# Choosing the rows of expert tiles with SyncE's registers instead of VectorE's tables, and new durations for the planner of the instruction order

## The chip, the cores and the metric

The kernel runs on one core of a Trainium2 chip. The metric is the device time of one execution in microseconds. A core has five engines with an instruction queue each: TensorE (PE; its weight loads are listed as PEld), VectorE (DVE), ScalarE (ACT), GpSimd (POOL) and SyncE (SP). Each works through its own queue in order, and they meet through semaphores. SyncE computes nothing on tensors: here it starts nearly all DMAs and has registers, on which its queue does whole-number arithmetic. GpSimd starts the indirect DMAs (scatters).

## The reference

A dynamic convolution is followed by a top-1 mixture of experts. The input x is (8, 3584, 192), in 8 heads of 24 columns; there are 8 experts with 1024 hidden columns.

```python
w = softmax(weight_gen)                         # (8, 3584, 8 heads, 7 taps)
attn[b, s, h, :] = sum_k w[b, s, h, k] * x_padded[b, s + k, h, :]
x = attn.reshape(28672, 192)
logits = x @ w_gate                             # 8 experts
e_idx = argmax(logits, axis=1)
gate_w = softmax(logits)[e_idx]
eom = 1 / (1 + exp(-(x @ w_output_gate)))
for e in range(8):
    mask = e_idx == e
    out[mask] = gate_w * eom[mask, e] * (relu(x[mask] @ w1[e]) @ w2[e])
```

Each row goes to one expert, so the rows of an expert have to be brought together before its matrix products, and how many there are is known only while the kernel runs.

## The kernel before

**The front.** The 28,672 rows are cut into 32 units of 896 rows (128 partitions of 7 rows, line 232 to 234). For a unit, softmax_steps (line 544) makes the seven weights of a row and head on VectorE and ScalarE. Seven products x times weight follow (product, line 532): five on GpSimd (tile gap) and two on VectorE for most units. From unit 7 on VectorE adds them up in PSUM (acc_steps, line 612: the add ps<-ps,gap for a product of GpSimd, ps<-ps,vt for one of its own); for the first seven units TensorE does it with an identity matrix. sum_steps (line 680) splits the sum into two float16 halves (tile rt), turns it with seven DMA transposes (tile gt, from unit 6 on), and TensorE makes the logits; lz is VectorE's read of them. Then VectorE finds the expert and TensorE the rank of each row among the rows of its expert (tile rk: columns 0 to 7 the rows ahead in the unit, columns 8 to 15 the unit's count for each expert). place_steps (line 835) adds the running total of each expert (tile base), and GpSimd scatters the 896 rows in seven indirect DMAs to a buffer in DRAM (srtd), in which each expert has 32,768 rows of its own.

**The tiles.** tile_steps (line 982) and tile_load (line 1003) load tiles of 512, 384, 256 or 128 rows of one expert: meta (row numbers and scales), xT (the rows, transposed by the DMA), and the expert's weights in float16 halves (wa or late, and wb). TensorE multiplies by w1 (gemm1_unit, line 1018); ScalarE takes relu into hh and VectorE the rest into hl (evac_steps, line 1031), which frees the PSUM bank; TensorE multiplies by w2 (gemm2_group, line 1040), ScalarE scales into ys, and GpSimd scatters to the output.

**Which tile comes next.** How many tiles of which size are taken after which unit is fixed when the kernel is written (plan_rounds, line 27): 76 tiles with 29,312 rows. Which expert a tile is of depends on the data. round_table (line 878) works that out on VectorE, on one partition: for R tiles of T rows it makes the 8 x R table of "expert e has T rows more" (gg), a running sum of it limited to R (cs), which of the R tiles is which expert's (ge), the first row of each (ti, row 1) and the expert's number by a shift of the row (ti, row 0, line 925). tile_load reads both numbers from SBUF into SyncE's registers with value_load (lines 1005 and 1006). After the last unit, VectorE also counts the 128-row tiles that are still left for a loop behind the planned ones (line 947).

**The waits.** A tile load must come after the scatters that write its rows. In before it waits for all scatters that stand ahead of it in the order (list(state["writers"]), line 997).

**The order.** Each engine's queue is written out by hand by a small planner. Every step of the work is a generator, a Chain with a rank and a time; Order.step (line 88) goes on with the chain that can start first, by rank among equals. Paced (line 138) and Queue (line 107) wrap the engines: each call adds the instruction and advances the engine's planned time by a duration from vector_cost, scalar_cost, gpsimd_cost, tensor_cost and sync_cost (lines 178 to 213), n being the elements of a partition. So these numbers are nothing that the chip sees, but they set in what order the instructions stand in each queue. Two tiles at a time are loaded ahead while the front runs (AHEAD, line 1260), four afterwards.

**The end.** When all 32 units are through, tile pools are exchanged, more PSUM banks are given to the products, and the tiles that are left run by themselves. Eight DMAs write a block of empty rows behind each expert's rows (pad, line 994).

Of the kernel before, what the change touches and what calls it, by code (L numbers as in the profile page):

```python
# [11 lines left out]
F32 = mybir.dt.float32  # L12
I32 = mybir.dt.int32
AF = mybir.ActivationFunctionType
ALU = mybir.AluOpType
# [5 lines left out]
RMAX = 24  # L21
SHIFT = 15
NE = 8
# [32 lines left out]
def constants():  # L56

    ident = np.eye(P, dtype=np.float32)
    upper = np.triu(np.ones((P, P), np.float32), 1)
    r = np.arange(RMAX, dtype=np.float32)  # L60
    rr = np.tile(r[:, None], (1, 9))
    need = [T * r for T in (128, 256, 384, 512)]
    e8 = np.arange(8, dtype=np.float32) - 8.0
    flat = np.concatenate([rr.ravel(), *need, e8]).astype(np.float32)
    return np.concatenate([ident, upper, np.tile(flat[None], (P, 1))], axis=1)
# [41 lines left out]
class Queue:  # L107
# [6 lines left out]
    @property  # L114
    def t(self):
        if self.host is not None:
            return self.host.t
        return max(self.moved, self.issued + self.lead)

# [86 lines left out]
def sync_cost(name, args, kwargs):  # L206
# [6 lines left out]
    return n / 360e3 * (1.25 if name == "dma_start_transpose" else 1.0)  # L213
# [4 lines left out]
def kernel(ctx: ExitStack, tc: tile.TileContext, x, wg, wgate, wogate, w1, w2, cst, out):  # L218
# [69 lines left out]
    f_mx = few[:, 80:136]  # L288
    f_lim = few[0:1, 189:190]

    f_next = few[0:1, 136:152].rearrange("p (e r) -> p e r", r=2)
    f_z = few[0:1, 152:170].rearrange("p (e r) -> p e r", r=2)
    f_done = f_next[:, :, 0]
    f_ex = ps[:, 2536:2538].bitcast(I32)
    f_rr = ps[0:1, 2512 : 2512 + RMAX]

    rest_free = [(0.0, 3904), (0.0, 1344)]
    mx_free, few_free, sq_free = [0.0], [0.0], [0.0]
# [44 lines left out]
    cf = cp.tile([P, cst.shape[1]], F32, name="cf")  # L343
    nc.scalar.dma_start(out=cf, in_=cst)
# [14 lines left out]
    o = 256  # L359
    rr = cf[0:1, o : o + RMAX * 9].rearrange("p (a b) -> p a b", b=9)  # L360
    o += RMAX * 9
    need = {}
    for k in (128, 256, 384, 512):
        need[k] = cf[0:1, o : o + RMAX]
        o += RMAX
    nc.vector.tensor_copy(f_e8, cf[:, o : o + 8])
# [3 lines left out]
    for e in range(NE):  # L370
        nc.vector.memset(base[:, e : e + 1], float(e * CAP - 1))
        nc.vector.memset(f_done[:, e : e + 1], float(e * CAP))


    cs = cp.tile([1, 1 + 8 * RMAX], F32, name="cs")
    nc.vector.memset(cs[:, 0:1], 0.0)
    nc.vector.memset(f_z[:, 8, :], float(DUMMY))
    nc.vector.tensor_copy(f_rr, rr[:, :, 0])
# [9 lines left out]
    state = {"base": base, "writers": [], "t": 0, "weights": 0, "rounds": 0}  # L388

# [154 lines left out]
    def softmax_steps(u):  # L544

        w4 = wloads[u]
        mxb = f_mx.unsqueeze(2).broadcast_to([P, NV, K])
        yield from take(mx_free, V)
# [21 lines left out]
        mx_free.append(od.cur.t)  # L570
# [109 lines left out]
    def sum_steps(u):  # L680
# [84 lines left out]
        od.add(place_steps(u), (RANK_C, u, 0), V)  # L765

# [67 lines left out]

    def place_steps(u):
# [11 lines left out]
        d["rk_home"].append((od.cur.t, d["rk_at"]))  # L847
        d["ranked"] = True
        if u in plan:
            od.add(round_steps(u), (RANK_R, u), V)  # L850
        else:
            state["rounds"] += 1
# [20 lines left out]
        d["sent"] = True  # L873
        d["sent_t"] = od.cur.t + 2.5
        rt_free.append((d["sent_t"], d["ri"]))


    def round_table(r, T, R, tail, bs):

        nm = f"{r}"  # L880
        rT = need[T][:, 0:R].unsqueeze(1).broadcast_to([1, 8, R])
        if R > 2:
            n = R
            nx = sp.tile([1, 8, RMAX], F32, tag="nx", bufs=1, name=f"nx{nm}")[:, :, 0:R]
            z = sp.tile([1, 9, RMAX], F32, tag="z", bufs=1, name=f"z{nm}")[:, :, 0:R]
            V.memset(z[:, 8, :], float(DUMMY))
            V.tensor_tensor(out=nx, in0=f_done.unsqueeze(2).broadcast_to([1, 8, R]), in1=rT, op=ALU.add)
            state["step"] = None
            yield V
        else:  # L890
            if state.get("step") != T:
                state["step"] = T if R == 2 else None
                if R == 2:
                    V.tensor_scalar(f_next[:, :, 1], f_done, float(T), None, op0=ALU.add)
                    yield V
            n = 2 if state["step"] == T else 1
            nx, z = f_next[:, :, 0:n], f_z[:, :, 0:n]

        gg = sp.tile([1, 8 * RMAX], F32, tag="gg", bufs=1, name=f"gg{nm}")[:, 0 : 8 * R]
        V.scalar_tensor_tensor(out=gg.rearrange("p (e r) -> p e r", r=R), in0=bs[0:1, :].unsqueeze(2).broadcast_to([1, 8, R]), scalar=0.0 if tail else 1.0 - T, in1=nx[:, :, 0:R], op0=ALU.add, op1=ALU.is_ge)  # L900
        yield V

        if state.get("limit") != R:
            V.memset(f_lim, float(R))
            state["limit"] = R
        V.tensor_tensor_scan(out=cs[:, 1 : 1 + 8 * R], data0=gg, data1=f_lim.broadcast_to([1, 8 * R]), initial=0.0, op0=ALU.add, op1=ALU.min)
        yield V
        cx = cs[:, 0 : 1 + 8 * R : R]

        V.scalar_tensor_tensor(out=z[:, 0:8, :], in0=cx[:, 0:8].unsqueeze(2).broadcast_to([1, 8, n]), scalar=-float(T), in1=nx, op0=ALU.mult, op1=ALU.add)  # L910
        ge = sp.tile([1, RMAX, 9], F32, tag="ge", bufs=1, name=f"ge{nm}")[:, 0:R, :]
        V.tensor_tensor(out=ge, in0=cx.unsqueeze(1).broadcast_to([1, R, 9]), in1=f_rr[:, 0:R].unsqueeze(2).broadcast_to([1, R, 9]), op=ALU.is_le)
        yield V
        n = 1 if R > 2 else n
        V.scalar_tensor_tensor(out=f_next[:, :, 0:n], in0=cx[:, 1:9].unsqueeze(2).broadcast_to([1, 8, n]), scalar=float(T), in1=z[:, 0:8, 0:n], op0=ALU.mult, op1=ALU.add)
        V.tensor_tensor(out=ge, in0=ge, in1=z[:, :, 0:R].rearrange("p e r -> p r e"), op=ALU.mult)
        yield V
        if R > 8:
            ti = sp.tile([1, 2, RMAX], I32, tag="til", bufs=1, name=f"ti{nm}")
        else:  # L920
            ti = sp.tile([1, 2, 8], I32, tag="ti", bufs=NU // 2 + 6, name=f"ti{nm}")
        with nc.allow_low_precision(reason="whole numbers"):
            V.tensor_reduce(out=ti[:, 1, 0:R], in_=ge, axis=AX, op=ALU.max)
        yield V
        V.tensor_scalar(ti[:, 0, 0:R], ti[:, 1, 0:R], SHIFT, None, op0=ALU.arith_shift_right)
        yield V
        return ti
# [3 lines left out]
    def round_steps(u):  # L931

        found, bs = [], U[u]["base"]
        yield V, lambda: state["rounds"] == u
        for k, (T, R) in enumerate(plan[u]):
            tail = u == NU - 1 and k == len(plan[u]) - 1
            pads = None
            if tail:
                pads = sp.tile([1, NE], I32, tag="bi", name="bi")
                bf = sp.tile([1, NE], F32, tag="bf", name="bf")  # L940
                V.tensor_scalar(bf, bs[0:1, :], 1.0, None, op0=ALU.add)
                yield V
                V.tensor_copy(pads, bf)
            ti = yield from round_table(f"{u}_{k}", T, R, tail, bs)
            for i in range(R):
                found.append((T, ti, i, pads if i == 0 else None))
        if u == NU - 1:

            more = sp.tile([1, NE], F32, tag="more", bufs=1, name="more")
            state["done"] = cp.tile([1, NE], F32, name="done")  # L950
            V.tensor_copy(state["done"], f_done)
            V.tensor_tensor(out=more, in0=bs[0:1, :], in1=f_done, op=ALU.subtract)
            yield V
            V.tensor_scalar(more, more, 128.0, None, op0=ALU.add)
            yield V
            morei = sp.tile([1, NE], I32, tag="morei", bufs=1, name="morei")
            V.tensor_copy(morei, more)
            yield V
            V.tensor_scalar(morei, morei, 7, None, op0=ALU.arith_shift_right)
            yield V  # L960
            V.tensor_copy(more, morei)
            yield V
            left = sp.tile([1, 1], F32, tag="left", bufs=1, name="left")
            V.tensor_reduce(out=left, in_=more, axis=AX, op=ALU.add)
# [338 lines left out]
```

## Time and profile before

| what | value |
|---|---|
| times of three runs | 1226.5, 1228.21, 1228.29 us; median 1228.21 |
| profiled execution: time, span | 1230.08 us, 1228.0 us |
| mean granted TensorE clock | 0.974 |
| VectorE shift ti<-ti: shortest, median, longest | 129, 170, 3364 ns |
| DMA issues on SyncE: transposes gt, tiles xT | 182, 76 |
| HBM over the span | 194 GB/s |

How to read it: the span runs from the first to the last instruction of the profiled execution. "Busy" is the time in which an engine had an instruction running; a busy TensorE need not be at its full rate, for which the granted clock stands. A row such as `PE ps <- DVE hl: 34.4, 38, 2.6` says that TensorE stood idle ahead of instructions on the tile ps until an instruction of VectorE on hl ended: us in total, times, longest. In the timeline, the number in brackets is the idle time ahead of an instruction and what ended it; neighbouring instructions of one kind are merged (x5). Nearly all instructions have the line of a helper (L151, L125), so the tiles' names tell them apart: out<-in. SPq is SyncE's queue.

### The profile page before, as it was taken

How to read it: one execution, taken by the hardware profiler on the slowest of the kernel's cores; microseconds unless marked ns; L12 is line 12 of the kernel's file. 1: busy time of each engine (PE TensorE's matmuls, PEld its weight loads, DVE VectorE, ACT ScalarE, POOL GpSimd, SP SyncE). 2: the span in 40 equal slices, each digit the busy share in tenths (PEclk: the TensorE clock that was granted, in tenths of full speed). 3: DMA queues.
4: the chain of work that ended last, by engine and by line, in shares of the span. 5: the costliest groups of instructions: out<-in, count | busy, mean ns of one | idle time of the engine just before them, and what ended most of it. 6: DMA issues, size and time to landing. Idle time of an engine off the chain costs nothing.

```text
span 1228.0 us, 27900 instructions
## 1 busy us (share of the span) xinstructions
PE 1132.9 (92%) x9710; PEld 821.3 (67%) x9710; DVE 956.4 (78%) x2027; ACT 594.5 (48%) x1263; POOL 879.8 (72%) x778
## 2 busy tenths in 40 slices
PE   5988779899999999899999999899998999999997
PEld 2444448677666666676766666676666777988987
DVE  6898759899999898998998999899998663333331
ACT  3875345455555445454544454445544544344342
POOL 5668786668888788888888988888887663322222
PEclk9998989899999999999999999999999999999999
DMA  9998378999989869698769759997777679889992
GB/s 281 284 283 288 131 237 196 262 277 250 247 232 240 206 182 248 150 262 211 213 191 229 208 154 244 231 234 188 207 203 185 178 219 278 235 255 330 272 310 80
DMA packets 278047, 279.73 MB, mean 228 GB/s; under 512 B 211479, under 2 KB 236808, under 8 KB 277905
## 3 DMA queue, kind: packets, MB, share of 16 engines
q1 hardware_dynamic: 256016, 233.35, 69.1%
q0 software_dynamic: 21744, 44.30, 13.3%
q8 instruction: 76, 1.25, 0.4%
q14 instruction: 67, 0.54, 0.1%
q10 hardware_dynamic: 144, 0.29, 0.1%
HBM read 177.07 MB, written 60.87 MB: 194 GB/s over the span
## 4 chain that ended last, share of the span: by engine, by line
PE 40%; DVE 26%; POOL 12%; issue 8%; DMA 7%; SPq 3%; ACT 3%; POOLq 0%; DVEq 0%; ACTq 0%
PE ps L151 40%; DVE ps L151 11%; POOL gap L151 6%; DVE hl L151 5%; POOL srtd L151 3%; SPq L125 3%; DMA srtd<-rt,posi 2%; POOL out_dram L151 2%; DMA wa<-wd 2%; DVE rt L151 2%; DMA gt<-rt 1%; DVE vap L151 1%; ACT rt L151 1%; DVE ti L151 1%; DVE vt L151 1%
## 5 line engine op out<-in xcount | busy, mean ns | idle before, releaser
L151 PE MATMUL ps<-xT,wa 128*128 128x512 f16 (+3 forms) x2440 | 493.0, 350 | 42.7 <-DVE hl L151 33.3
L151 PE MATMUL ps<-wb,hh 128*128 128x192 f16 x3664 | 478.9, 248 | 4.8 <-DVE hl L151 4.8
L151 PE MATMUL ps<-wb,hl 128*128 128x192 f16 x1832 | 454.1, 248 | 0.1
L151 DVE SCALAR_TENSOR_TENSOR hl<-ps,hh 128x512 f16<-128x512 f32 (+1 forms) x472 | 307.5, 665 | 156.3 <-ACT hh L151 155.9
L151 POOL TENSOR_TENSOR gap<-x,w 128x960 f32<-128x960 f32 (+5 forms) x268 | 360.0, 1368 | 37.1 <-DVE lz L151 9.2
L151 ACT ACTIVATE hh<-ps 128x512 f16<-128x512 f32 (+1 forms) x472 | 272.1, 582 | 226.1 <-PE ps L151 223.5
L151 PEld LDWEIGHTS <-wa 128*128 128x128 f16 x2440 | 226.5, 99 | 226.7 <-issue 48.8
L151 PEld LDWEIGHTS <-hh 128*128 128x128 f16 x3664 | 337.0, 99 | 50.5 <-issue 9.4
L151 POOL DMA_INDIRECT out_dram<-ys,meta x216 | 214.5, 993 | 193.6 <-ACT ys L151 146.3
L151 POOL DMA_INDIRECT srtd<-rt,posi x224 | 229.0, 1022 | 87.0 <-issue 56.4
L151 DVE TENSOR_TENSOR ps<-ps,gap 128x1344 f32<-128x1344 f32 x125 | 194.2, 1554 | 21.8 <-POOL gap L151 21.8
L151 ACT ACTIVATE ys<-ps,sc 128x192 f32<-128x192 f32 x229 | 96.3, 421 | 221.0 <-PE ps L151 160.5
L151 PEld LDWEIGHTS <-hl 128*128 128x128 f16 x1832 | 180.9, 99 | 0.6 <-DVE hl L151 0.3
L151 PE MATMUL ps<-gap,cf 128*128 128x512 f32 x168 | 72.9, 569 | 3.2 <-DVE vap L151 3.2
L151 PE MATMUL ps<-vap,cf 128*128 128x512 f32 (+1 forms) x126 | 58.2, 603 | 13.5 <-DVE vap L151 12.9
L151 POOL TENSOR_TENSOR gap<-halo,w 128x1152 f32<-128x1152 f32 (+4 forms) x38 | 60.4, 1589 | 13.2 <-issue 5.7
L151 DVE SCALAR_TENSOR_TENSOR rt<-ps,sx,rt 128x448 f16<-128x448 f32 x64 | 57.9, 908 | 10.4 <-ACT rt L151 5.8
L151 PE MATMUL ps<-xT,late 128*128 128x128 f16 (+2 forms) x600 | 56.6, 251 | 0.0
L151 ACT ACTIVATE rt<-ps 128x1344 bf16<-128x1344 f32 x32 | 41.3, 1291 | 28.2 <-issue 18.3
L151 PEld LDWEIGHTS ps<-gap,cf 128*128 128x128 f32 x168 | 31.4, 199 | 34.8 <-issue 25.6
L151 PEld LDWEIGHTS ps<-vap,cf 128*128 128x128 f32 x126 | 24.9, 208 | 38.7 <-issue 22.9
L151 ACT ACTIVATE rt<-ps,sx 128x1344 f16<-128x1344 f32 x32 | 44.2, 1380 | 9.6 <-DVE isx L151 7.6
(123 smaller groups left out, 841.8 us busy)
## 6 DMA issues: line engine op xcount, KB each, us to landing
wb<-wd SPq DMA_DIRECT2D x76, 768.5 KB
wa<-wd SPq DMA_DIRECT2D x61, 768.0 KB
x<-in_x_dram SPq DMA_DIRECT2D x32, 672.0 KB
late<-wd SPq DMA_DIRECT2D x15, 768.0 KB
wa<-wd SPq DMA_DIRECT2D x61, 128.0 KB
w<-in_wg_dram SPq DMA_DIRECT2D x32, 196.0 KB
wd<-wpb SPq DMA_DIRECT2D x8, 768.5 KB
st<-in_w_dram SPq DMA_DIRECT2D x8, 768.0 KB
```

Of the source, the lines that this page charges most:

```text
L125: r = f(*args, **kwargs)
L151: r = f(*args, **kwargs)
```

## The change

Five things change.

1. SyncE keeps one register for each expert: key[e] = (rows waiting << 11) + (first row / 128). After each unit, ScalarE writes the unit's eight counts, times 2048, as whole numbers to SBUF (count_steps); SyncE loads them and adds them to the keys (counted).
2. pick(T) takes the largest of the eight keys, so the expert with most rows waiting, or an empty tile if no expert has T rows, moves that expert's key on by T rows, and leaves the first row in a register for tile_load. round_table and VectorE's closing count are gone; end_of writes the blocks of empty rows, and turns_left counts the tiles left, which come back through one DMA from a table of numbers.
3. A tile load waits for the scatters up to the unit for which it was picked (U[u]["writers"]), not for all that stand ahead of it.
4. The planner's durations for VectorE, ScalarE, GpSimd and the DMAs are new, and it counts SyncE's register work (spend).
5. softmax_steps has two places for f_mx in PSUM instead of one, and the table of constants is 264 columns wide when loaded.

The plan of sizes, the ranks and the other constants stay. The diff, cut to its core:

```diff
 def vector_cost(name, args, kwargs):
     n = largest(args, kwargs)
-    return 0.06 + n / 156.0 if name == "reciprocal" else 0.07 + n / 960.0
+    return 0.15 + n / 156.0 if name == "reciprocal" else 0.15 + n / 960.0
...
 def scalar_cost(name, args, kwargs):
-    return (0.19 if "accum_out" in kwargs else 0.1) + largest(args, kwargs) / 1200.0
+    own = max(0.2, 0.12 + largest(args, kwargs) / 1050.0)
+    return own + (0.2 if "accum_out" in kwargs else 0.0) + (0.0 if isinstance(kwargs.get("scale", 1.0), float) else 0.1)
...
 def gpsimd_cost(name, args, kwargs):
     if name == "indirect_dma_start":
-        return 1.2 if LOCK else 1.04
+        return 1.28
...
-    return (0.14 if LOCK else 0.06) + largest(args, kwargs) * (0.0022 if kwargs.get("op") == ALU.add else 0.00174)
+    return 0.19 + largest(args, kwargs) * (0.0022 if kwargs.get("op") == ALU.add else 0.00178)
...
-    return n / 360e3 * (1.25 if name == "dma_start_transpose" else 1.0)
+    return n / 310e3 * (1.5 if name == "dma_start_transpose" else 1.0)
...
+    def counted(cnt):
+        R.reg_load(came, cnt[0:1, 0:NE])
+        for e in range(NE):
+            R.reg_alu(key[e], key[e], came[e], ALU.add)
+        SP.spend(0.6)
+
+    def pick(T):
+        R.reg_mov(best, (T - 1 << HAVE) + (DUMMY >> ROW))
+        for e in range(NE):
+            R.reg_alu(best, best, key[e], ALU.max)
+        for e in range(NE):
+            R.reg_alu(came[e], key[e], best, ALU.is_ge)
+            R.reg_alu(came[e], came[e], (T >> ROW) - (T << HAVE), ALU.mult)
+            R.reg_alu(key[e], key[e], came[e], ALU.add)
+        R.reg_alu(best, best, low, ALU.bitwise_and)
+        SP.spend(1.1)
+        return R.snap(best, min_val=0, max_val=DUMMY >> ROW)
...
+    def count_steps(u):
+        cnt = U[u]["cnt"] = sp.tile([1, NE], I32, tag="cnt", bufs=CNT, name=f"cnt{u}")
+        S.activation(cnt, U[u]["rk"][0:1, 8:16], AF.Copy, scale=float(1 << HAVE))
+        rank_read(u)
...
-    def round_table(r, T, R, tail, bs):
...
     def round_steps(u):
-        found, bs = [], U[u]["base"]
-        yield V, lambda: state["rounds"] == u
...
-            ti = yield from round_table(f"{u}_{k}", T, R, tail, bs)
+        yield SP, lambda: state["rounds"] == u and "counted" in U[u]
+        od.cur.t = max(od.cur.t, U[u]["counted"])
+        yield SP
+        counted(U[u]["cnt"])
+        found, subs = [], [(T, k) for k, (T, n) in enumerate(plan.get(u, ())) for _ in range(n)]
+        for T, k in subs:
...
+            yield SP
+            found.append((T, pick(T), u))
...
-            d = tile_load(state["t"], T, ti, i, list(state["writers"]), ka, kb)
+            d = tile_load(state["t"], T, at, U[u]["writers"], ka, kb)
...
-        e = SP.value_load(ti[0:1, 0, i : i + 1], min_val=0, max_val=NE - 1)
-        row = SP.value_load(ti[0:1, 1, i : i + 1], min_val=0, max_val=DUMMY + 4 * P - T)
+        R.reg_alu(hit, at, SHIFT - ROW, ALU.logical_shift_right)
+        e = R.snap(hit, min_val=0, max_val=NE - 1)
+        row = at * (1 << ROW)
```

More of the change, by code (lines that the diff above doesn't have):

```diff
@@ L59, in constants @@
     upper = np.triu(np.ones((P, P), np.float32), 1)
[L60 to L62 removed]
     e8 = np.arange(8, dtype=np.float32) - 8.0
[L64 removed]
+    turns = np.arange(TURNS, dtype=np.int32).view(np.float32)
+    flat = np.concatenate([e8, turns])
     return np.concatenate([ident, upper, np.tile(flat[None], (P, 1))], axis=1)
@@ L873, in place_steps @@
         d["sent"] = True
+        d["writers"] = list(state["writers"])
         d["sent_t"] = od.cur.t + 2.5
         rt_free.append((d["sent_t"], d["ri"]))
-    def round_table(r, T, R, tail, bs):
[L880 to L927, printed above, removed]
@@ L947, in round_steps @@
-        if u == NU - 1:
[L949 to L964, printed above, removed]
-            yield V
-            lefti = state["left"] = sp.tile([1, 1], I32, tag="lefti", bufs=1, name="lefti")
-            V.tensor_copy(lefti, left)
@@ L968, in round_steps @@
-        state["rounds"] += 1
+        yield SP, lambda: state["rounds"] == u and "counted" in U[u]
[4 more added lines that the diff above has]
+        for T, k in subs:
+            if u == NU - 1 and k == len(plan[u]) - 1 and "ended" not in state:
+                state["ended"] = True
+                for e in range(NE):
+                    yield SP
+                    end_of(e)
+                    od.cur.t = od.now
+            yield SP
+            found.append((T, pick(T), u))
@@ L1280 @@
 GT = 1
+CNT = 4
 TR_U = 6
```

108 lines of the change are left out of this document (53 added, 55 removed).

## The prediction

> **What bounds the kernel now.** I read the page first, then the busy times by stage, the chain, the waits of each engine in the middle stage, and at last the timeline around single stalls.
>
> ```profile
> span 1228.0 us, 27900 instructions
> PE 1132.9 (92%) x9710; PEld 821.3 (67%) x9710; DVE 956.4 (78%) x2027; ACT 594.5 (48%) x1263; POOL 879.8 (72%) x778
> ```
>
> Busy times by stage (us, then busy us and instructions of PE, PEld, DVE, ACT, POOL; granted clock; DMA):
>
> ```profile
> 260.00:960.00 700.00, 660.01 (x5704) 471.56 (x5702) 652.56 (x1361) 345.36 (x773) 602.83 (x529) 0.98 0.82 214
> 0.00:260.00 260.00, 212.78 (x1251) 132.44 (x1252) 205.36 (x472) 139.84 (x264) 183.25 (x153) 0.93 0.85 249
> ```
>
> The last long piece of the chain:
>
> ```profile
> 963.13 254.02 PE ps L151 x2694
> ```
>
> The kernel ends in 254.02 us of TensorE without a break, so a backlog of tiles is there when the front (attention, routing) stops. The time is therefore TensorE's work plus TensorE's idle time plus what the slow clock costs. A front that merely runs faster gains nothing; only removed gaps on TensorE do. They lie ahead of 963 us: 260 - 212.78 = 47 us idle in the first stage, 700 - 660.01 = 40 us in the middle one, and a granted clock of 0.93 and 0.98, worth up to 0.07 x 260 = 18 and 0.02 x 700 = 14 us.
>
> What TensorE waits for in the middle stage (us, times, longest):
>
> ```profile
> PE ps L151 <- DVE hl L151: 34.4, 38, 2.6
> ```
>
> So 34.4 of the 40 us are VectorE's second half of an evacuation (hl, line 1034) coming late. VectorE is busy 652.56 of 700 us and runs in order: what stands ahead of an hl delays TensorE. Two things do. The first is the last operation of a routing table (line 925):
>
> ```profile
> 500.86 3.36 DVE L151 TENSOR_SCALAR ti<-ti 1x2 int32<-1x2 int32 x1
> 501.49 2.70 POOL L151 TENSOR_TENSOR gap<-x,w 128x576 f32<-128x576 f32 x2
> 504.14 1.55 DVE L151 TENSOR_TENSOR ps<-ps,gap 128x1344 f32<-128x1344 f32 x1
> ...
> 506.08 0.67 DVE L151 SCALAR_TENSOR_TENSOR hl<-ps,hh 128x512 f16<-128x512 f32 x1
> 506.68 1.54 DVE L151 TENSOR_TENSOR ps<-ps,gap 128x1344 f32<-128x1344 f32 x1
> 506.80 1.24 PE L151 MATMUL ps<-xT,wa 128*128 128x512 f16 x5 [2.65 <-DVE hl L151]
> ...
> 508.14 0.67 DVE L151 SCALAR_TENSOR_TENSOR hl<-ps,hh 128x512 f16<-128x512 f32 x1
> ```
>
> A shift of two numbers lasts 3.36 us and ends when GpSimd's pair of products ends (501.49 + 2.70 = 504.19); hl comes late, TensorE stands 2.65 us, and then runs slow:
>
> ```profile
> 506.00:513.00 7.00, 5.38 (x28) 3.19 (x28) 6.93 (x8) 1.38 (x3) 6.21 (x6) 0.76 0.71 174
> ```
>
> 7 x (1 - 0.76) = 1.7 us more are lost to the clock. The second thing is a product of GpSimd that comes later than the order of VectorE's instructions expects:
>
> ```profile
> 568.52 2.73 POOL L151 TENSOR_TENSOR gap<-x,w 128x576 f32<-128x576 f32 x2
> 571.28 1.57 DVE L151 TENSOR_TENSOR ps<-ps,gap 128x1344 f32<-128x1344 f32 x1 [1.71 <-POOL gap L151]
> 572.75 0.68 DVE L151 SCALAR_TENSOR_TENSOR hl<-ps,hh 128x512 f16<-128x512 f32 x1
> 573.49 1.83 PE L151 MATMUL ps<-xT,wa 128*128 128x512 f16 x4 [2.62 <-DVE hl L151]
> ```
>
> In the middle stage VectorE waits so in all:
>
> ```profile
> DVE ps L151 <- POOL gap L151: 21.8, 18, 2.4
> ```
>
> **The change, part by part.** *Tables off VectorE.* All of round_table goes. The shift by form, and the first and last of its six other common kinds (busy us, mean ns):
>
> ```profile
> L151 DVE TENSOR_SCALAR ti<-ti 1x2 int32<-1x2 int32 x20 | 18.6, 928 | 0.1
> L151 DVE TENSOR_SCALAR ti<-ti 1x1 int32<-1x1 int32 x7 | 0.9, 132 | 0.0
> ```
>
> ```profile
> L151 DVE SCALAR_TENSOR_TENSOR ps<-cs,ps 1x16 f32<-1x16 f32 (+1 forms) x54 | 8.9, 165 | 1.5
> L151 DVE SCALAR_TENSOR_TENSOR gg<-base,ps 1x16 f32<-1x16 f32 (+1 forms) x27 | 4.0, 150 | 0.0
> ```
>
> The two-number shift waits, the one-number shift does not: 20 x (928 - 132) ns = 15.9 us of waiting. The six kinds hold 33 us over 32 units, about 24 us in the middle stage. VectorE's load there falls from 652.6 to about 611 us. On TensorE's path I count the two gaps that stand behind a shift of over 3 us, 2.65 and the one here:
>
> ```profile
> 698.78 1.28 PE L151 MATMUL ps<-xT,wa 128*128 128x512 f16 x5 [2.59 <-DVE hl L151]
> ```
>
> With 1.7 us of slow clock each that is 5.2 + 3.4 = 8.6, and near 1 us for the shorter shifts: **9.5 us**. Ends: 5 if other work of VectorE slips into the place, 11 if every trace of it goes.
>
> *The order's durations.* GpSimd's work in the middle stage:
>
> ```profile
> L151 POOL TENSOR_TENSOR gap<-x,w 128x768 f32<-128x768 f32 (+5 forms) x195 | 260.6, 1363 | 3.0 <-issue 1.6
> L151 POOL DMA_INDIRECT srtd<-rt,posi x159 | 155.8, 980 | 52.2 <-issue 43.1 <-ACT rt L151 5.9 <-DVE hl L151 0.6
> L151 POOL DMA_INDIRECT out_dram<-ys,meta x150 | 149.9, 1000 | 41.7 <-issue 20.3 <-ACT ys L151 8.6 <-ACT hh L151 5.2
> ```
>
> 159 scatters are 159 / 7 = 22.7 units, 30.8 us each. GpSimd is busy 602.8 us and 43.1 + 20.3 us in issue: 95%. The order of before gives an indirect DMA 1.04 us; 0.98 and 0.30 of issue make 1.28, the new value. Over 309 of them the old order is 74 us short, 3.3 us in every unit, and for the two products above it expects 2.46 us where 2.73 are seen. So it sets VectorE's adds ahead of an hl at a time when the product isn't there. Seven TensorE gaps of over 1 us follow such a wait, the first and the last being
>
> ```profile
> 419.69 1.63 PE L151 MATMUL ps<-xT,wa 128*128 128x512 f16 x4 [1.98 <-DVE hl L151]
> 944.98 1.24 PE L151 MATMUL ps<-xT,wa 128*128 128x512 f16 x5 [1.48 <-DVE hl L151]
> ```
>
> in sum 12.5 us; three of them are of about 2 us or more, with 1.7 of clock each: 17.5. An order that knows the product's time can put the hl first, but GpSimd stays as full as it was; I take half: **8.7 us** (ends 0 and 17.5). What is left of hl's 34.4, 34.4 - 5.2 - 12.5 = 16.7 us, are small gaps of a VectorE at 93%; at 87% I take a third: **5 us** (ends -5, since any new order makes gaps of its own, and 16).
>
> *Fewer writers for a tile load.* Each load waited for every scatter placed so far; now it waits for those up to its own unit. SyncE's queue in the middle stage, and its register work and TensorE's waits on weights in the first stage:
>
> ```profile
> SPq L125 <- DMA srtd<-rt,posi: 128.6, 34, 10.4
> ```
>
> ```profile
> L125 SPq FUSED_REGOPS  x548: 37/51/178, 141.8 to 1194.9; - x183
> L125 SPq TENSOR_LOAD <-ti x152: 261/278/935, 141.1 to 1190.5; - x152
> ```
>
> ```profile
> PE ps L151 <- DMA wa<-wd: 8.1, 2, 5.9
> ```
>
> Most of the 128.6 us (5.7 a unit) goes, but two tiles loaded ahead hide it in the middle stage: nothing. In the first stage tiles are scarce and the 8.1 us lie open, with a share of the 18 us of slow clock. I take half of the wait and 2 of clock: **6 us** (ends 0 and 13).
>
> *Start.* Between these rows eleven of twenty small instructions go, 1.55 x 11 / 20 = **0.9 us**, on VectorE's way to the first matmul:
>
> ```profile
> 4.73 0.17 DVE L366 COPY ps<-cf 128x8 f32<-128x8 f32 x1 [4.73 <-DMA cf<-in_cst_dram]
> ...
> 6.28 0.57 DVE L151 TENSOR_REDUCE ps<-w 128x56 f32<-128x392 f32 x1
> ```
>
> *What is added.* A choice of a tile is 34 register operations: at 51 ns 1.7 us, 1.75 times a unit (896 rows of 512). The counts add one to eight loads of 278 ns and eight additions, 0.7 to 2.6 us. That is 3.7 to 5.6 us a unit on SyncE, against 5.7 of waiting and 2 x 0.278 x 1.75 = 1.0 of loads that go: hidden. SyncE now waits for ScalarE's count; behind it stand tile loads, x and w loads and the transposes of gt, for which TensorE's logits and then VectorE's lz wait. ScalarE's count is like
>
> ```profile
> L151 ACT CAST posi<-pos 128x7 int32<-128x7 f32 x23 | 4.4, 192 | 5.6 <-DVE pos L151 5.6
> ```
>
> 0.19 us a unit on an engine busy 345 of 700 us: nothing. The second place for f_mx and the pads' earlier writing: nothing, beside the 254 us. The number of extra turns now comes by a DMA behind SyncE's last issue at about 1195 us, 22 us ahead of TensorE's end at 963.13 + 254.02: nothing. For new gaps I give back **2 us**.
>
> Sum: 9.5 + 8.7 + 5 + 6 + 0.9 - 2 = 28 us off a span of 1228.0, so 1200. The profiled execution took 1230.1, 2.1 us more than its span and 1.9 more than the median of 1228.2, so the median forecast is **1200**.
>
> A rule beside this: the gap of 2.65 us was followed by a clock of 0.76. The Trainium skill (TensorE: Matmul & The Clock Gate, Part 1) has the clock drop after an idle window of about 3.4 us, longer than any of these gaps; if they cost no clock, 3.4 us of the first term and 2.6 of the second leave the sum, and it is 1206. The trace, with its 0.76, speaks against it.
>
> **The rivals.** *GpSimd holds the pace.* It is at 95%, and nothing is taken from it; a VectorE with room then waits for products instead, and the hl behind them stay late. For it: 21.8 us of such waits. Against: the hl needn't stand behind. Then 9.5 + 0.9 + 1 remain: 1217.
>
> *The durations mislead.* 506.68 with 1.54 is followed at 508.14: 1.46 from start to start. The new 0.15 + n/960 is the record's length; the old 0.07 + n/960 is the spacing. Without the tables' 8 or 9, about 1361 / 22.7 - 8.5 = 51 instructions a unit x 0.08 = 4.1 us that VectorE doesn't need, so the order sees it at 611 / 22.7 + 4.1 = 31.0 us of 30.8, takes it for the bound and spreads work wrongly. The 8.7 and 5 go: 1214. The Trainium skill (Perfetto Trace Analysis, the lifecycle of a DVE instruction) says that a record runs until the write is acknowledged while the next instruction may begin earlier, which speaks for this rival; the spacing agrees.
>
> *Slower: SyncE holds up the front.* If the queue stands at the count, the gt transposes come late, and VectorE stands at lz:
>
> ```profile
> DVE lz L151 <- PE ps L151: 7.6, 6, 3.6
> ```
>
> Today that is six times 1.3 us. A VectorE stall costs TensorE 2.65 / 3.36 = 0.8 of it. At 2 us in each of 22.7 units it is 36 us, less 28: 1236. It decides above 28 / 22.7 / 0.8 = 1.5 us a unit. Against it: the 5.7 us a unit that SyncE gains.
>
> *The change doesn't do what it says.* The plan of tile sizes is untouched, and the rows of each expert, counted from the inputs, fill 228 blocks of 128 where 229 are planned: one empty tile and no extra turn either way. The work is the same; no case of its own.
>
> **How the numbers follow.** Forecast 0.58; GpSimd 0.16; durations 0.10; gains eaten by new gaps, no change, 0.03; SyncE 0.13. A change under 0.2% (2.5 us) can't be told from none here. Faster 0.84, same 0.03, slower 0.13. The upper ends together give 11 + 17.5 + 16 + 13 + 0.9 = 58, so 1170; near all of them at once has 0.05, and the low end is 1174. The high end, 1230, takes in all but the slower rival.
>
> **What would show it.** Right: VectorE without ti, ge, cs and with about 890 us busy; PE's wait for hl in the middle stage near 15 us; clock 0.99 there; SyncE's wait for srtd near nothing; the unbroken end longer than 254 us or starting earlier. GpSimd rival: the waits of VectorE for gap above 21.8. SyncE rival: lz waits of over 1.5 us a unit. Wrong: TensorE's idle time ahead of the end still 87 us.

## The result, and the profile after

The changed kernel took 1261.18 us (median of 4, 1257.99 to 1264.33) where the kernel before took 1228.25 (4 runs, 1226.5 to 1228.31): a ratio of 1.0272 [1.0244, 1.0299]. I had forecast 1200 and a range of 1174 to 1230. One thing is needed to read the runs below: on the chips of the first two sets (e1 to e8) the kernel before itself takes 1288 and 1298 us and TensorE and VectorE of the kernels traced there stand for issue, so ratios are compared only within a set there, and no conclusion rests on those two sets' ratios alone.

The page after, span and busy times:

```profile
span 1256.2 us, 27736 instructions
PE 1127.0 (90%) x9710; PEld 817.4 (65%) x9710; DVE 910.0 (72%) x1721; ACT 599.2 (48%) x1295; POOL 876.5 (70%) x778
```

VectorE lost 46 us of work, less than forecast: about 890 was said and 910 came (the groups that the prediction lists, 18.6 + 0.9 us of shifts and 33 us of the six other kinds, would give 904). TensorE's work is the same and its idle time is 1256.2 - 1127.0 = 129 us, 95 before; the mean granted clock is 0.958, 0.974 before. By stage (columns as before):

```profile
0.00:260.00 260.00, 213.62 (x1318) 136.48 (x1319) 193.28 (x410) 141.25 (x277) 180.64 (x153) 0.93 0.82 245
260.00:960.00 700.00, 638.22 (x5519) 453.86 (x5517) 604.71 (x1120) 340.47 (x765) 575.24 (x505) 0.97 0.80 208
960.00:1256.00 296.00, 275.19 (x2878) 227.03 (x2875) 111.98 (x193) 117.48 (x254) 120.66 (x121) 0.96 0.82 238
```

The last stage of the kernel before, to set beside the third row:

```profile
960.00:1228.00 268.00, 260.13 (x2760) 217.35 (x2758) 98.48 (x196) 109.26 (x228) 93.75 (x98) 1.00 0.83 243
```

The first stage is as it was. The middle one has 62 us of idle TensorE where there were 40, and the last 21 where there were 8. TensorE's waits over the whole span:

```profile
PE ps L155 <- DMA wa<-wd: 73.7, 14, 13.7
...
PE ps L155 <- DVE hl L155: 4.5, 5, 1.7
```

and the wait for hl before:

```profile
PE ps L151 <- DVE hl L151: 38.1, 40, 3.4
```

These lines hold most of the result. The waits for hl that I set out to remove went from 38.1 us to 4.5, more than forecast, though not for the reason forecast (see below); the waits for a tile's weights went from 8.1 to 73.7. The chain of waits shows how one of them comes about (start, us, what; "SPq L129" is SyncE's queue at the recording helper):

```profile
876.38 2.38 DMA srtd<-rt,posi
...
883.47 1.47 SPq L129
...
892.13 1.25 SPq L129
...
896.19 6.67 DMA wa<-wd
902.90 15.41 PE ps L155 x109
```

and SyncE's timeline of the same place gives the names:

```profile
882.96 0.34 SPq L129 DMA_DIRECT2D wb<-wd  x1
883.47 9.92 SPq L129 DMA_TRANSPOSE gt<-rt  x7
893.78 0.40 SPq L129 DMA_DIRECT2D meta<-srtd  x1
894.34 1.64 SPq L129 DMA_TRANSPOSE xT<-srtd  x1
896.19 1.15 SPq L129 DMA_DIRECT2D wa<-wd  x2
```

The unit's rows land at 878.8. One tile is loaded, seven transposes of another unit take 9.9 us of the queue, the second tile's weights are issued at 896.19, and TensorE starts on them 6.7 us later. There is no tile in stock between "its rows are there" and "TensorE needs it". In the last stage the gap has another place in the queue:

```profile
1030.55 0.35 SPq L129 DMA_DIRECT2D wb<-wd  x1
1049.01 6.99 SPq L129 DMA_DIRECT2D srtd<-pad  x8
1071.25 0.41 SPq L129 DMA_DIRECT2D meta<-srtd  x1
```

For 40 us no tile is loaded; between the rows lie the 23 choices of the last unit and the pads. TensorE then stands 13.7 us.

### The profile page after: what moved, and what is told of

The parts are those of the page before. It is cut to its first block, busy times and chain, and to the rows that moved or that the text cites. A ratio compares the mean times of both kernels' runs of the same rounds, so it can differ in the third digit from the quotient of the medians.

```text
span 1256.2 us, 27736 instructions
## 1 busy us (share of the span) xinstructions
PE 1127.0 (90%) x9710; PEld 817.4 (65%) x9710; DVE 910.0 (72%) x1721; ACT 599.2 (48%) x1295; POOL 876.5 (70%) x778
## 3 DMA queue, kind: packets, MB, share of 16 engines
q0 software_dynamic: 21744, 44.30, 12.5%
## 4 chain that ended last, share of the span: by engine, by line
PE 63%; SPq 10%; DMA 10%; issue 6%; POOL 5%; DVE 4%; ACT 1%; POOLq 0%; DVEq 0%; ACTq 0%
PE ps L155 63%; SPq L129 7%; DMA wa<-wd 5%; POOL gap L155 3%; DMA w<-in_wg_dram 2%; DMA srtd<-rt,posi 1%; DVE vap L155 1%; POOL out_dram L155 1%; POOL srtd L155 1%; DMA gt<-rt 1%; DVE ps L155 1%; DVE wa L155 1%; DMA wd<-wa 1%; SPq L397 1%; SPq L398 1%
## 5 line engine op out<-in xcount | busy, mean ns | idle before, releaser
L155 PE MATMUL ps<-xT,wa 128*128 128x512 f16 (+3 forms) x2560 | 513.9, 351 | 78.0 <-DMA wa<-wd 73.7
L155 PE MATMUL ps<-wb,hh 128*128 128x192 f16 x3664 | 472.7, 247 | 0.0
L155 DVE SCALAR_TENSOR_TENSOR hl<-ps,hh 128x512 f16<-128x512 f32 (+1 forms) x472 | 310.7, 671 | 201.1 <-ACT hh L155 197.3
L155 PEld LDWEIGHTS <-wa 128*128 128x128 f16 x2560 | 235.3, 99 | 270.7 <-DMA wa<-wd 77.9
L155 DVE TENSOR_REDUCE ps<-w 128x56 f32<-128x392 f32 x64 | 36.2, 566 | 27.4 <-DMA w<-in_wg_dram 23.5
L155 ACT ACTIVATE rt<-ps 128x1344 bf16<-128x1344 f32 x32 | 41.3, 1291 | 30.2 <-DVE ps L155 22.8
L155 PEld LDWEIGHTS ps<-gap,cf 128*128 128x128 f32 x168 | 32.0, 199 | 33.4 <-issue 25.2
L155 PE MATMUL ps<-gm,gt 128*128 128x32 f16 x672 | 26.8, 180 | 23.9 <-DVE ps L155 9.3
```

What stands on the lines that cost most here:

```text
L155: r = f(*args, **kwargs)
```

## The experiments

**Is it SyncE's register work, or the order's durations?** The first theory, A, put the loss down to SyncE standing at ScalarE's count and working out choices; B to the new durations. Three kernels take them apart. The first is the kernel before with only the five new cost formulas:

```diff
-    return ... else 0.07 + n / 960.0
+    return ... else 0.15 + n / 960.0      (and the other four of the change)
```

> The kernel before with only the five new duration formulas; tables, writers and f_mx stay. Theory A (SyncE's queue: it stands at the count and at the choices, and the tile loads behind them come late): the tables aren't read before a load, so nothing stands ahead of the loads, TensorE's wait for weights stays near the 8 us of before, its wait for hl falls from 42 to about 25 us, and the time is 1205 to 1222. Theory B (the new durations set the tile loads later in SyncE's queue, with or without registers): TensorE waits over 40 us for weights and the time is above 1245.

It took 1323.36 us beside 1288.09, 1.0281 [1.0206, 1.0356]. The second is the changed kernel with the five old formulas.

> The changed kernel with the five duration formulas of before. Theory A: still slow, 1245 to 1270, with TensorE waiting 50 us or more for weights and SyncE some 60 us for the count. Theory B: at most 1228, with the wait for weights near 8 us.

1295.62 us, 1.0059 [1.0029, 1.009]. The third is the changed kernel with its choices behind the unit's scatters:

```diff
-        od.add(round_steps(u), (RANK_R, u), SP)
+        od.add(round_steps(u), (RANK_A, -1, u), SP)
-        yield SP, lambda: state["rounds"] == u and "counted" in U[u]
+        yield SP, lambda: state["rounds"] == u and "counted" in U[u] and "sent" in U[u]
```

> The changed kernel, with the count and the choices of a unit made only after its scatters stand in the order, and ranked behind the tile loads, so that SyncE seldom waits for the count and loads come first after the last unit. Theory A: SyncE's wait for the count falls from some 76 us to under 15, TensorE's wait for weights from 74 to under 25, the 13.7 us gap behind the last unit's 23 choices goes, and the time is 1195 to 1220. Theory B: no more than the 13.7 us gap and its slow clock go, so 1240 or more.

1302.34 us, 1.0122 [1.0063, 1.0182]. TensorE's wait in the three traces, in that order:

```profile
PE ps L151 <- DMA wa<-wd: 64.7, 14, 12.6
```

```profile
PE ps L155 <- DMA wa<-wd: 16.7, 3, 8.9
```

```profile
PE ps L155 <- DMA wa<-wd: 73.8, 11, 19.6
```

As the cause of these waits A falls: without any register work they are there, and with the wait for the count moved away they stay. SyncE does stand at the load of the counts, 83.8 us in the changed kernel, but only 6.3 us in e3, whose waits for wa are the same. They come with the durations. What a long run of choices does in the last unit is another matter (e17).

**The shift that waits.** The two-number shift made as two one-number shifts, in the kernel before:

```diff
-        V.tensor_scalar(ti[:, 0, 0:R], ti[:, 1, 0:R], SHIFT, ...)
+        for lo, hi in ((0, 1), (1, 2)) if R == 2 else ((0, R),):
+            V.tensor_scalar(ti[:, 0, lo:hi], ti[:, 1, lo:hi], SHIFT, ...)
```

> The kernel before, with the shift of two numbers made as two shifts of one number each, nothing else. If the two-number form waits for GpSimd's products and that costs TensorE what the prediction's first term says, no shift lasts over 0.4 us and the time is 1216 to 1222. The rival, that the stall is absorbed elsewhere: the shifts are short and the time stays within 3 us of 1228.

1294.13 us, 1.005 [1.0014, 1.0086]. The groups of its trace show the waiting gone (20 at 928 ns before):

```profile
L151 DVE TENSOR_SCALAR ti<-ti 1x1 int32<-1x1 int32 x47 | 4.8, 132 | 0.1
```

16 us of waiting were taken from VectorE and no time was gained in that set: 6 us more, outside both expectations. It was a first hint that VectorE is not what sets the pace, and no more than that, since the kernel before has no trace on that chip.

**Why do durations cause waits?** The order that the kernel writes out keeps its own clock, so it can be read off when a tile's load is written how many chosen tiles are left in stock, and when its first matmul is written how long TensorE is reckoned to stand for it. For loads between 260 and 960 us of that clock (mean stock; reckoned stand over all tiles), beside what the trace of the same kernel then measured:

| kernel | stock, tiles | reckoned stand, us | measured wait for wa, us |
|---|---|---|---|
| before | 3.9 | 5.7 | 8.1 |
| changed | 0.42 | 76.0 | 73.7 |
| e1, durations alone | 0.43 | 110.5 | 64.7 |
| e8, VectorE's formula alone | 0.42 | 100.3 | 94.0 |
| e6, TensorE reckoned slower | 0.89 | 2.1 | 18.6 |
| e7, old durations | 4.7 | 0.4 | 1.8 |

With the new durations the order takes the front for the slower side. It then writes each tile at the place where its rows are just there, and since the front's and the tiles' instructions share queues, the chip cannot run ahead of what is written. That is theory C; D, its rival, is that longer durations misplace single instructions. The next set, first the changed kernel unaltered:

> The changed kernel, unaltered, as the measure for the others on the same chip. Both theories expect the ratio of its first timing, 1.024 to 1.030, and TensorE's wait for wa of 70 us or more.

1292.08 us beside 1298.08, 0.9966 [0.994, 0.9992], with a wait for wa of 72.4 us: the waits repeat, the loss of time does not, on a chip on which the kernel before is slowed more. Both theories had expected the loss again. Then a longer matmul in the order's reckoning (2100 in place of 2400):

> The changed kernel, but the order reckons a matmul 2400/2100 = 1.14 times as long; nothing else is altered, all the new durations stay. Theory C, no stock: with the new durations the order believes that VectorE and GpSimd, and so the front, are the slower side, and writes TensorE's tiles and the units of the front so that a tile is used as soon as its rows are there; by the order's own clock a load then leaves 0.4 tiles in stock (3.9 in the order of before) and TensorE stands 76 us at the starts of tiles (5.7 before). With the longer matmul that reckoned stand falls to 2 us. C expects TensorE's wait for wa under 20 us and a ratio to before of 1.000 or less. Rival D, wrong places: the longer VectorE and GpSimd durations set single instructions in bad places whatever TensorE's are; it expects a wait for wa of 40 us or more and a ratio of 1.015 or more.

1296.05 us, 0.9986 [0.996, 1.0013]. The trace's waits:

```profile
PE ps L155 <- issue: 39.3, 45, 4.9
PE ps L155 <- DMA wa<-wd: 18.6, 3, 14.0
PE ps L155 <- DVE hl L155: 17.4, 22, 2.6
```

Stock does remove the waits for wa, as C says, but other waits took their place, so stock is not the whole of it. Old durations with the choices behind the scatters (the edits of e2 and e3 together):

> The registers with the old durations (1.006 when run before), and with the choices of tiles set behind the unit's scatters and ahead of other work of the same time. C: the order's reckoned stand at tile starts is 0.4 us, and SyncE no longer stands at ScalarE's count; the wait for wa falls from 16.7 to under 8 us and the 11.8 us that TensorE stood behind the count go; ratio 0.98 to 0.995. D expects no more than the registers' own effect: 1.00 to 1.006.

1282.26 us, 0.9872 [0.983, 0.9914]. And VectorE's formula alone in the kernel before:

> The kernel before with only VectorE's duration of an instruction altered, 0.15 + n/960 for 0.07 + n/960. C: this formula alone makes the order believe that VectorE is the bound (reckoned stand at tile starts 100 us, stock 0.4); it expects most of the loss of all the new durations together (1.028): 1.015 to 1.035, with over 40 us of waits for wa. D's weaker form, that the loss comes from GpSimd's or SyncE's durations, expects 0.995 to 1.008 and a wait for wa below 20 us.

1375.3 us, 1.0589 [1.0528, 1.065], with the largest wait of all:

```profile
PE ps L151 <- DMA wa<-wd: 94.0, 14, 14.6
```

So one formula, 0.08 us more for each VectorE instruction, is enough to empty the stock. The loss is above the 1.015 to 1.035 that C expected, and above that of all five formulas in e1, on another chip.

**The kernel before again.** On a chip where it took 1226.92.

> The kernel before, unaltered, for a trace of it on a chip of the experiments, on which it has taken 1288 to 1298 us where the first chip took 1228. In the traces there TensorE and VectorE stand for issue (11.7 to 39.3 us and 28.7 to 68.1 us; 0 and 0.6 on the first chip). Theory E, instructions arrive late there: a TensorE that is always busy pays for each such stand, one that waits for loads pays less; expected are 30 us or more of issue ahead of TensorE, still under 15 us of waits for wa, and a busy end that takes more than its 254 us. Rival: the matmuls themselves take longer there; then the mean of a 128x512 matmul is 4 per cent above its 382 ns and issue stays under 10 us.

1228.1 us, 0.9997 [0.9978, 1.0015]. This chip showed no issue ahead of TensorE, so the run can't tell what slows the chips of the first two sets. It stays open.

**Stock alone.** On that same chip, e7 with a matmul reckoned 1.04 times as long, and the changed kernel with choices behind the scatters and 2000 in place of 2400:

> The registers, the old durations, the choices behind the scatters (0.987 before) and a matmul reckoned 2400/2300 = 1.04 times as long, so that by the order's clock a load leaves 6.6 tiles in stock (4.7 without). Theory C, stock: more of it can only help; no waits for wa, ratio 0.975 to 0.99. Rival D, places: the stock was enough at 4.7 and any other order only moves the gaps; 0.985 to 1.00.

> The changed kernel with all its new durations, the choices behind the scatters, and a matmul reckoned 1.2 times as long (2.1 tiles in stock by the order's clock, TensorE's reckoned stand 1.4 us). C: with the stock restored the new durations do no harm; waits for wa under 15 us and a ratio within 0.01 of the same kernel with old durations, 0.98 to 0.997. D: the new durations cost by themselves; 1.00 or more though the waits for wa are gone.

1284.06 us, 1.0472 [1.0432, 1.0512], and 1287.35, 1.0468 [1.0423, 1.0512]. C failed in both. The waits for wa are gone (0.6 and 1.1 us), and the time is worse. e10 differs from e7 only in the reckoned matmul, but e7 was not run on this chip: whether the chip or the edit turns 0.9872 into 1.0472 is open. VectorE's waits in the middle stage of the first of them:

```profile
DVE ps L155 <- DMA w<-in_wg_dram: 43.4, 10, 8.6
DVE ps L155 <- POOL gap L155: 22.2, 17, 4.9
```

and TensorE's, over the span:

```profile
PE ps L155 <- DVE hl L155: 63.3, 40, 10.0
```

VectorE stands at the first operation of a softmax for its w; in the trace of before it never did so. That operation writes f_mx. With two places for f_mx a softmax may be written as soon as its w is reckoned to land: by the order's clock 4.5 us behind the landing, 25.4 in the order of before. The real load is later, and an hl queued behind it waits up to 10 us.

**Fewer writers, alone** (the kernel before with the list of writers kept for each unit):

```diff
-            d = tile_load(state["t"], T, ti, i, list(state["writers"]), ka, kb)
+            d = tile_load(state["t"], T, ti, i, U[u]["writers"] if u < NU - 1 else list(state["writers"]), ka, kb)
```

> The kernel before with one part of the change alone: a tile's load waits for the scatters up to its own unit. My prediction gave this 6 us of the 28 (ends 0 and 13), in the first stage. It expects SyncE's wait for srtd to fall from 170 to under 100 us, TensorE's wait for wa of 8.1 us to halve, ratio 0.993 to 0.997. Rival: two tiles loaded ahead hide all of it; the wait of SyncE falls, ratio 0.998 to 1.002.

1226.91 us beside 1226.92, 1.0 [0.9981, 1.0018]. Not even SyncE's wait fell (170.7 before):

```profile
SPq L125 <- DMA srtd<-rt,posi: 169.8, 35, 14.0
```

**One place for f_mx.** Four kernels on one chip, on which before took 1227.89, each with

```diff
-    mx_free, few_free, sq_free = [(0.0, 80), (0.0, 136)], [0.0], [0.0]
+    mx_free, few_free, sq_free = [(0.0, 80)], [0.0], [0.0]
```

from the changed kernel, from e10, from e2 and from e11:

> The changed kernel with one place for f_mx, as before. Theory F, the second place: it lets a softmax start when its w is only just reckoned to be there (by the order's clock 11.6 us after its landing, 25.4 in the order of before; 22.0 here); VectorE's wait for w falls from 23.5 to under 10 us. Theory C, stock: the stock stays at 0.4 tiles, so the waits for wa stay at 60 us or more, and the ratio at 1.02 to 1.04. If the second place were the whole cause, the ratio would fall to 1.00 or less.

> Registers, old durations, choices behind the scatters, a matmul reckoned 1.04 times as long (1.047 before), now with one place for f_mx: stock 5.8 tiles, w reckoned 26.5 us ahead of its use. F and C together: no wait of VectorE for w, none of TensorE for wa, hl under 40 us; ratio 0.975 to 0.995. Theory A, SyncE's register work and waits make w late: VectorE still stands 20 us or more at w and the ratio stays above 1.02.

> The change without its durations and without the second place for f_mx: registers, counts and fewer writers, the choice set where the change sets it. By the order's clock TensorE stands 12 us at the starts of tiles and w is there 21 us ahead. F and C: 0.985 to 1.005, with waits for wa of 10 to 20 us. Theory A: SyncE stands at ScalarE's count and ratio above 1.01.

> The new durations, the choices behind the scatters, a matmul reckoned 1.2 times as long (1.047 before), with one place for f_mx: stock 1.8 tiles, w reckoned 14.6 us ahead. F and C: the wait for w falls from 43 to under 15 us, waits for wa under 15, ratio 0.99 to 1.015. D, the new durations put single instructions in bad places: 1.03 or more with hl above 50 us though w is in time.

| kernel | us | ratio | wa wait | hl wait |
|---|---|---|---|---|
| e13, changed | 1271.47 | 1.0383 [1.033, 1.0437] | 85.8 | 1.7 |
| e14, old durations, stock | 1267.78 | 1.0314 [1.0286, 1.0341] | 6.3 | 53.7 |
| e15, registers only | 1248.7 | 1.0167 [1.0149, 1.0185] | 19.7 | 35.9 |
| e16, new durations, stock | 1258.93 | 1.0246 [1.0217, 1.0274] | 4.2 | 52.7 |

e13 and e15 differ in nothing but the durations: 1.0383 - 1.0167 = 0.0216, 26.5 us (22.8 between the two medians), and their TensorE waits show what it is:

```profile
PE ps L155 <- DMA wa<-wd: 85.8, 12, 18.4
```

```profile
PE ps L155 <- DVE hl L155: 35.9, 37, 3.2
PE ps L155 <- DMA wa<-wd: 19.7, 2, 10.4
```

e13 and e16 have the same durations and ran on the same chip: with stock in the order the wait for wa falls from 85.8 to 4.2 us and the ratio by 0.0137, so C has a part of the cause. The rest of e16 is no clean test of D, since VectorE still stands 18.7 us at w in its middle stage, more than was expected.

The second place seems to cost 0.016 to 0.022 where there is stock (e10 to e14, e11 to e16) and to help where there is none (1.0272 to 1.0383 for the changed kernel), but each of these steps compares two chips. Against both F and C, e14 with stock and w in time is far above 1; why it is also above e15, from which it differs in the place of the choices and the reckoned matmul, is open. And e15, the registers without anything else, still loses, though its VectorE has 611.20 us to do in the middle stage where 652.56 were. Its VectorE's largest wait in the middle stage, and GpSimd's DMA groups there:

```profile
DVE ps L155 <- POOL gap L155: 46.1, 28, 4.5
```

```profile
L155 POOL DMA_INDIRECT srtd<-rt,posi x167 | 163.6, 979 | 55.0 <-issue 44.8 <-ACT rt L155 5.0 <-DMA srtd<-rt,posi 1.5
L155 POOL DMA_INDIRECT out_dram<-ys,meta x149 | 148.8, 999 | 44.6 <-issue 21.7 <-ACT ys L155 8.0 <-DVE isx L155 5.5
```

With its 598.94 us of work GpSimd is at (598.9 + 44.8 + 21.7) / 700 = 95%, as before. VectorE's new room is spent waiting for GpSimd, 46.1 us where there were 21.8; in e14 it is 51.0.

**The two last causes.** e15 with the last unit's choices behind tile loads due at the same time, and that kernel with GpSimd making four of seven products in every second unit. The second has no room of its own for VectorE's third column of weights, which overwrites numbers of the routing and of another unit, so what it computes from there on is not the reference's; it has the same 9710 matmuls, moves the same 279.6 MB, and 26 instructions went from GpSimd to VectorE.

```diff
-        od.add(round_steps(u), (RANK_R, u), SP)
+        od.add(round_steps(u), (RANK_R, u) if u < NU - 1 else (RANK_A, -1, u), SP)
```

```diff
-POOL = (5,)
+POOL = (5, 4)
```

> The registers alone, and the last unit's choices behind the tile loads that are due at the same time. Theory L, the last choices: the gap of 10.4 us and the slow clock behind it go, the end is unbroken; ratio 1.000 to 1.008. Rival: the choices are needed for those loads; the gap stays above 7 us and the ratio at 1.012 or more. VectorE's wait for GpSimd stays near 46 us and hl near 33 us by both.

> The same, and in every second unit GpSimd makes four of the seven products of a unit and VectorE three (five and two before), so that GpSimd has about 29 us less to do in the middle part and VectorE takes part of its new room for it. Theory G, GpSimd holds the pace: the front gets faster, VectorE's wait for products falls under 30 us and TensorE's hl wait under 25 us; ratio 0.98 to 0.997 and at least 0.005 below the kernel before it in this call. Rival V, VectorE's room is needed: hl 33 us or more and a ratio no lower than that kernel's.

1234.28 us, 1.0065 [1.0044, 1.0086], and 1211.74, 0.9881 [0.9859, 0.9902]. The end of the first one's chain:

```profile
926.53 291.26 PE ps L155 x3000
```

The gap in the last stage is gone: theory L, 0.0102 or 12.5 us (14.4 between the medians; e15 and e17 ran on the same chip). The middle stage of e17, its busy times, then VectorE's and TensorE's waits there:

```profile
260.00:960.00 700.00, 656.74 (x5639) 468.61 (x5637) 610.47 (x1159) 345.02 (x792) 597.86 (x527) 0.98 0.81 215
```

```profile
DVE ps L155 <- POOL gap L155: 45.4, 28, 4.4
```

```profile
PE ps L155 <- DVE hl L155: 31.8, 30, 3.2
```

and the same three of e18:

```profile
260.00:960.00 700.00, 669.12 (x5839) 479.45 (x5838) 641.76 (x1217) 357.24 (x815) 582.15 (x517) 0.99 0.83 218
```

```profile
DVE ps L155 <- POOL gap L155: 11.2, 16, 2.0
```

```profile
PE ps L155 <- DVE hl L155: 12.3, 15, 1.5
```

With 16 us less on GpSimd and 31 us more on VectorE, 200 more matmuls fit into the same 700 us, and hl falls to 12.3. Theory G holds for these kernels with the old durations: GpSimd sets the front's pace. The edit also lets the planner write another order, so how much of the 0.0184 is GpSimd's is not shown; that both waits fall while VectorE works more is what speaks for G. In the changed kernel it is not so: VectorE waits only 5.5 us for products in the middle stage, and GpSimd is at (575.2 + 40.9 + 15.6) / 700 = 90%.

## Why the prediction was wrong

**Tables off VectorE (9.5 us): failed.** The work left VectorE as said (652.6 to 611 us in e15), the shift's waiting too, but hl stayed at 33.4 us in the middle stage of e15 and 31.8 in e17, against 34.4. I had read "hl comes late because VectorE is at 93%" from a busy share; GpSimd, at 95% with its issue, was the one to ask. My rival "GpSimd holds the pace" had this mechanism; I gave it 0.16, and its 1217 left out the two costs below. Its sign, waits for gap above 21.8 us, shows in e15 (46.1) but not in the changed kernel (5.5), where TensorE stands for weights instead. The 5 us of small gaps failed with it. That hl fell to 4.5 us in the changed kernel is luck and no success of this term: the fall goes with the durations (1.7 us in e13, and 16.9 in e1, which keeps the tables), while e15, the same registers with the old durations, has 35.9.

**The order's durations (8.7 us gained): wrong in sign, and the step that failed most.** (The working has a small slip: eight gaps of over 1 us follow a wait for a product, not seven; one of 1.02 us at 447.95 is left out, so 13.5 for 12.5 us.) They cost 0.0216, 26.5 us (e13 against e15). The rival "the durations mislead" had the cause, a VectorE reckoned at 31.0 us a unit, and priced it as a gain that does not come. I did not follow the reckoning to the tiles: an order that takes the front for the slower side keeps no tile in stock. The rule cited there, that a record runs on while the next instruction may begin (the Trainium skill, Perfetto Trace Analysis, the lifecycle of a DVE instruction), agrees with the trace of before, where a record of 1.54 us is followed after 1.46. e8 shows what the record's length as a cost does to this order: 94.0 us of waits.

**What is added: hidden. Failed in one place.** A choice is cheaper than I said: in the changed kernel's trace it is four fused operations and some moves, 1.25 us from one to the next (628.88 to 630.13) where I had 1.7. Rows of two of its lines and of the load of all eight counts:

```profile
L395 SPq FUSED_REGOPS  x76: 185/185/195, 112.9 to 1068.5; - x76
...
L397 SPq FUSED_REGOPS  x76: 241/241/245, 113.4 to 1069.0; - x76
...
L386 SPq TENSOR_LOAD <-cnt x32: 531/552/1540, 63.9 to 1033.0; - x32
```

But I divided the work evenly over the units. The last unit has 23 choices and the pads in one piece, 40 us of queue. I had put the pads "beside the 254 us"; they and the choices were not beside it but ahead of the loads on which it lives: 12.5 us.

**The second place for f_mx: nothing. Failed.** It takes away the lead of w: 43.4 us of VectorE's waits in e10, and 23.5 in the changed kernel against 5.2 in e13. What that costs in time is not shown, since e13, without the second place, is no faster on its chip.

**Fewer writers (6 us): nothing** (e12, 1.0). SyncE's wait for srtd, which I wanted near nothing, is still 81.3 us in the changed kernel and 154.9 in e15. **Start (0.9 us): right in kind, too small**; the first reduction of VectorE came 2.3 us sooner, half of it because the table, which is loaded smaller, lands at 3.58 where it was 4.73 (rows before, at 4.73 and 6.28, are in the prediction):

```profile
3.58 0.17 DVE L357 COPY ps<-cf 128x8 f32<-128x8 f32 x1 [3.58 <-DMA cf<-in_cst_dram]
3.75 0.12 DVE L362 MEMSET base<- 128x1 f32 x8
3.98 0.57 DVE L155 TENSOR_REDUCE ps<-w 128x56 f32<-128x392 f32 x1
```

**The slower rival** needed 1.5 us of lz waits a unit. In the changed kernel they are

```profile
DVE lz L155 <- PE ps L155: 21.1, 15, 6.0
```

over about 22 units, under 1 us each: the kernel did get slower, but not there, and not through ScalarE's count (e3).

The account in ratios: registers with the last choices moved, +0.0065 (e17); last choices, +0.0102 (e15); durations, +0.0216 (e13); the second place together with them, -0.0111 (the changed kernel). Their sum is 0.0272 by construction, each step is known to 0.002 to 0.006, and the last step compares two chips. Open are e17's 0.0065 (its SyncE still stands 44.6 us at the load of the counts, a rival that no run tests by itself), the sign of the last step, and why the changed kernel took no longer than the kernel before on the chip of e5.

## What to carry to other kernels

Before counting a gain on a busy engine, ask what the other nearly full engine allows: here VectorE at 93% and GpSimd at 95% looked alike, and only moving work off GpSimd paid. Where instructions are ordered by a reckoned clock, true durations are not the aim; what counts is which side the order takes for the slower one, because that decides whether work is kept in stock for the engine that must never stand. Stock alone isn't enough: e14 and e16 had it and were still 3.1% and 2.5% slower. And a queue's added work is to be priced where it comes in one piece, not as a mean.

## What the runs showed of the hardware

SyncE fuses register operations: the 34 of a choice show as four records of 185 to 241 ns (medians) and a few moves, where records of 51 ns in the trace of before had led me to one by one and 1.7 us. Eight registers load in one instruction of 552 ns. And the same program's speed differs by chip: 1223.88 to 1301.92 us for the kernel before over all sets. On the slower chips TensorE stands for issue in every kernel traced, 39.3 us in e6; in e9, on another chip, it has no such wait. The kernel before was not traced on the slower ones.
